# Decode attention over two KV caches: slots of eight heads with 64 KB runs, products in place, one V buffer

## The chip, the cores and the metric

The kernel runs on one core of one Trainium2 chip. The metric is the device time of one execution in microseconds (us); lower is better. The kernel before takes 2577.59 us (median of 3 runs, 2576.91 to 2578.84).

## The reference

Two independent attention blocks, A and B, of the same shapes; their outputs stand side by side. All data are bf16. There is one query token per batch, so each byte of K and V is used once.

```python
B, Sq, D = 8, 1, 1024
H, Sk, Dh = 32, 4096, 128
q = (x @ wq).reshape(B, Sq, H, Dh).transpose(0, 2, 1, 3)
scores = einsum("bhqd,bhkd->bhqk", q, k_cache) * Dh ** -0.5
p = softmax(scores, axis=-1)
o = einsum("bhqk,bhkd->bhqd", p, v_cache)
y = o.transpose(0, 2, 1, 3).reshape(B, Sq, H * Dh) @ wo      # for A and for B
```

K and V of both blocks are 4 x 268 MB, wq and wo 4 x 8.4 MB.

## The kernel before

The program is built as lists of operations, one for each engine, in the order in which they are added (`Program`). Each operation names what it reads and writes and which PSUM banks it touches; from that the program works out the semaphore waits. An engine does its list in order. Stretches of the lists that repeat are emitted as loops (`rolled`).

**Slots.** The work is cut into slots. A slot is one batch and HP = 4 heads of one block, so there are NS = 128 of them. A head's 4096 tokens are spread over SEG = 32 partitions, T = 128 tokens each; four heads fill the 128 partitions. K of a slot is one DMA of 4 MB: 128 rows, each one run of 32 KB (`load_k`), and V likewise (`load_v`). There are two K buffers and two V buffers. All these DMAs are issued by SP, in the order of the list, each after the readers of its buffer are done.

**Scores.** For each half of a slot's tokens (`ch`, 64 tokens of each partition), DVE multiplies K by the query, which `make_qbc` has spread over the partitions, into `prod` (`multiply`, L348). PE adds 16 groups of 8 columns by matmuls with the identity into the PSUM bank `red` (`add_up`, L358), DVE adds the remaining 8 (`reduce`, L371).

**Softmax.** DVE takes the maximum of each partition, transposes blocks of 32 so that the maximum over a head's 32 partitions can be taken, and scales it (L376 to L381). ACT does four Exp instructions, one for each head on its 32 partitions (L385), which write `prob` and the row sums. `prob` has one column per head and is zero on the other heads' partitions, so that one matmul serves all four heads.

**Output.** `pv` does 32 matmuls, four side by side in column groups of the array, into `oacc` (L416). ACT copies it to `osb` (L405). `gather` adds its strips with the selection matrix `sel` (L438), `rowsum` and `invert` give one over the sum of the exps, and `heads` multiplies the two. After eight slots `permute`, `permuted` and `project` multiply with 512 rows of wo (`load_wo`, 1 MB). The last eight slots are projected at the very end, where V comes in four parts of 1 MB and wo in two.

**Order.** Slot n issues K(n) and V(n-1), multiplies its first half, finishes the second half and the softmax of slot n-1, gathers slot n-2, and does `pv` of slot n-1 last. A slot's chain therefore reaches into the next two slots. At the start the four halves of the two wq are loaded into the V and K buffers.

Of the kernel before, what the change touches and what calls it, by code (L numbers as in the profile page):

```python
# [145 lines left out]
def _build(nc, caches, out):  # L146
# [4 lines left out]
    HP = 4  # L151
# [9 lines left out]
    QT = 4  # L161
    NB = 2
    RS = 4
    assert Sq == 1 and Dh == 128 and Sk == 4096 and D == 1024 and H % HP == 0 and B == 8
    assert RS * H * Dh == T * Dh and R == NB * RS
# [3 lines left out]
    with es:  # L169
# [7 lines left out]

        ident = sb("ident", [128, 128], BF16)
        ones = sb("ones", [128, 128], FP32)
        sel = sb("sel", [128, TB, HP], FP32)  # L180
        xs = sb("xs", [B, NC, D], BF16)
        xT = sb("xT", [128, NC, R, B], BF16)
        qrow = sb("qrow", [128, 2, 512], BF16)
        qT = sb("qT", [128, NC, H * B], BF16)
        qbc = sb("qbc", [128, 2, QT, Dh], BF16)
        kbuf = sb("kbuf", [128, NB, T * Dh], BF16)
        vbuf = sb("vbuf", [128, NB, T * Dh], BF16)
        wob = sb("wob", [128, HP, D], BF16)
        prod = sb("prod", [128, 2, CT * Dh], BF16)
        score = sb("score", [128, 2, T], FP32)  # L190
        prob = sb("prob", [128, 2, T, HP], BF16)
        rmax = sb("rmax", [128, 2], FP32)
        tmax = sb("tmax", [128, 2, SEG], FP32)
        nmax = sb("nmax", [128, 2], FP32)
        bias = sb("bias", [128, 2], FP32)
        rsum = sb("rsum", [128, 2, HP], FP32)
        rl = sb("rl", [128, 2, HP], FP32)
        osb = sb("osb", [128, 2, 512], FP32)
        olate = sb("olate", [128, 2 * Dh], FP32)
        on = sb("on", [128, HP, B], BF16)  # L200
        onp = sb("onp", [128, HP, B], BF16)
        qg = sb("qg", [128, HP, B], BF16)
        pick = sb("pick", [40, 2, B], FP32)
        osum = sb("osum", [40, 512], FP32)
        asb = sb("asb", [40, 512], FP32)
        orow = sb("orow", [40, NC, 512], BF16)

        red = [ps(f"red{i}", [128, 512]) for i in range(2)]
        oacc = [ps(f"oacc{i}", [128, 512]) for i in range(2)]
        acc = ps("acc", [128, 512])  # L210
        accr = ps("accr", [128, 512])
        qps = [oacc[0], oacc[1]]
        bps = ps("bps", [128, 512])
        sps = ps("sps", [128, 512])

# [5 lines left out]
        for c in range(NC):  # L221
            dma("act", xs[:, c, :], caches[c][0].rearrange("b s d -> (b s) d"), [f"xs{c}"], f"x{c}")
# [5 lines left out]
        for j in range(4):  # L228
# [3 lines left out]
        P.add("pool", lambda e: e.memset(pick[:], 0.0), writes=["pick"])  # L232
        P.add("pool", lambda e: e.affine_select(
            out=pick[:], in_=pick[:], compare_op=ALU.not_equal, fill=1.0, base=0,
            pattern=[[-32, 2], [-1, B]], channel_multiplier=1), reads=["pick"], writes=["pick"])
        P.add("dve", lambda e: e.memset(prob[:], 0.0), writes=[f"prob{i}h{h}" for i in range(2) for h in range(HP)])
        P.add("dve", lambda e: e.memset(rsum[:], 0.0), writes=[f"rsum{i}h{h}" for i in range(2) for h in range(HP)])
        P.add("dve", lambda e: e.memset(olate[:], 0.0), writes=["olate"])
        P.add("dve", lambda e: e.memset(ones[:], 1.0), writes=["ones"])
        for i in range(2):  # L240
            P.add("dve", lambda e, i=i: e.memset(oacc[i][:], 0.0), banks=[f"oacc{i}"])
        P.add("dve", lambda e: e.memset(acc[:], 0.0), banks=["acc"])
        P.add("dve", lambda e: e.memset(accr[:], 0.0), banks=["accr"])

        ring = {"k": 0, "v": 0}
        bufs = {"k": kbuf, "v": vbuf}

        def slot(which):
            i = ring[which] % NB
            ring[which] += 1  # L250
            return i

        def load_wq(which, c, s):
            i = slot(which)
            w = bufs[which][:, i, :].rearrange("p (r n) -> p r n", r=RS)
            src = caches[c][3].rearrange("(p r) n -> p r n", r=R)[:, s * RS:(s + 1) * RS, :]
            dma("sp", w, src, [f"{which}{i}"], f"{which}{i}")
            return f"{which}{i}", w

        def make_xT(c):  # L260
            def emit(e):
                last = None
                for r in range(R):
                    last = e.matmul(sps[:, 256 + r * B:256 + (r + 1) * B], xs[:, c, r::R], ident[0:B, 0:B], start=True, stop=True)
                return last
            P.add("pe", emit, reads=[f"xs{c}", "ident"], banks=["sps"])
            P.add("dve", lambda e: e.tensor_copy(xT[:, c].rearrange("p r b -> p (r b)"), sps[:, 256:256 + R * B]),
                  writes=[f"xT{c}"], banks=["sps"])

        def q_part(c, s, name, w):  # L270
            def emit(e):
                last = None
                for r in range(RS):
                    for k in range(8):
                        q = k % 4
                        last = e.matmul(qps[k // 4][32 * q:32 * q + B, :], xT[:, c, s * RS + r, :], w[:, r, k * 512:(k + 1) * 512],  # L276
                                        start=(s == 0 and r == 0), stop=(s == R // RS - 1 and r == RS - 1), tile_position=(0, 32 * q))
                return last
            P.add("pe", emit, reads=[name, f"xT{c}"], banks=["oacc0", "oacc1"])
            if s < R // RS - 1:  # L280
                return
            for k in range(2):
                P.add("dve", lambda e, k=k: e.tensor_copy(qrow[:, k, :], qps[k][:]), writes=[f"qrow{k}"], banks=[f"oacc{k}"])  # L283
# [8 lines left out]
            P.add("pe", turn, reads=["qrow0", "qrow1", "ident"], banks=["bps"])  # L292
            P.add("dve", lambda e: e.tensor_copy(qT[:, c, :], bps[:, 0:H * B]), writes=[f"qT{c}"], banks=["bps"])

        def load_k(n):
            gi, b = divmod(n, B)
            c, g = divmod(gi, NG)
            i = kslot[n] = slot("k")
            src = caches[c][1][b, g * HP:(g + 1) * HP].rearrange("h (p t) d -> (h p) (t d)", t=T)
            dma("sp", kbuf[:, i, :], src, [f"k{i}"], f"k{i}")  # L300

        def load_v(m, parts):
            gi, b = divmod(m, B)
            c, g = divmod(gi, NG)
            i = slot("v")
            src = caches[c][2][b, g * HP:(g + 1) * HP].rearrange("h (p t) d -> (h p) (t d)", t=T)
            w = T * Dh // parts
            names = [f"v{i}"] + [f"vpart{k}" for k in range(1, parts)]
            for k in range(parts):
                dma("sp", vbuf[:, i, k * w:(k + 1) * w], src[:, k * w:(k + 1) * w], [names[k]], names[k])  # L310
            vslot[m] = (i, names)

        def load_wo(gi):
            c, g = divmod(gi, NG)
            src = caches[c][4][g * HP * Dh:(g + 1) * HP * Dh, :]
            if gi < NC * NG - 1:
                dma("sp", wob[:], src.rearrange("(p h) n -> p h n", p=Dh), ["wo"], "wo")
                return
            src = src.rearrange("(h p) n -> p h n", p=Dh)
            for k, name in enumerate(("wo", "wolate")):  # L320
                dma("sp", wob[:, 2 * k:2 * k + 2, :], src[:, 2 * k:2 * k + 2, :], [name], name)

        def pick_q(gi):
            c, g = divmod(gi, NG)
            P.add("pool", lambda e: e.tensor_copy(qg[:].rearrange("p h b -> p (h b)"), qT[:, c, g * HP * B:(g + 1) * HP * B]),
                  reads=[f"qT{c}"], writes=["qg"])

        def make_qbc(n):
            b0 = n % B
            i = (n // QT) % 2  # L330

            def emit(e):
                last = None
                for j in range(QT):
                    for hh in range(HP):
                        last = e.matmul(bps[hh * SEG:(hh + 1) * SEG, j * Dh:(j + 1) * Dh],
                                        qg[:, hh, b0 + j:b0 + j + 1].to_broadcast([128, SEG]), ident[:], start=True, stop=True,
                                        tile_position=(0, hh * SEG))
                return last
            P.add("pe", emit, reads=["qg", "ident"], banks=["bps"])  # L340
            P.add("act", lambda e: e.activation(qbc[:, i].rearrange("p i d -> p (i d)"), bps[:], ACTF.Copy),
                  writes=[f"qbc{i}"], banks=["bps"])

        def multiply(n, ch):
            ki, qi, i = kslot[n], (n // QT) % 2, ch % 2
            pv = prod[:, i, :].rearrange("p (t d) -> p t d", d=Dh)
            kv = kbuf[:, ki, ch * CT * Dh:(ch + 1) * CT * Dh].rearrange("p (t d) -> p t d", d=Dh)
            P.add("dve", lambda e: e.tensor_tensor(  # L348
                pv, kv, qbc[:, qi, n % QT, :].unsqueeze(1).to_broadcast([128, CT, Dh]), ALU.mult),
                reads=[f"k{ki}", f"qbc{qi}"], writes=[f"prod{i}"])  # L350
# [156 lines left out]
        def idle(k):  # L507
            if not k:
                return
# [207 lines left out]
```

## Time and profile before

| | before |
|---|---|
| median of 3 runs | 2577.59 us |
| the profiled execution's own time | 2578.69 us |
| its span | 2576.5 us |
| bytes moved by DMA | 1107.59 MB, mean 430 GB/s |
| share of the span in which the engine is busy | PE 62%, DVE 56%, ACT 15%, POOL 1% |
| multiply (L348), 128 x 8192 elements | 256 times 4420 ns |
| Exp (L385), 32 x 128 elements | 512 times 576 ns |
| mean granted TensorE clock | 0.789 of full speed |

The span is the time from the first to the last instruction of the program in the profile, and the profiled execution's own time lies 2.2 us above it. A row of a group gives the line, the engine, the operation, what is written and read, the shape, and the count; behind the bar stand the busy time in us, the mean duration of one in ns, and the idle time of the engine just before it, with what ended that. In a window's row stand its length, the busy time of PE, PE's weight loads, DVE, ACT and POOL with their counts, the granted clock, the busy share of the DMA engines, and GB/s.

### The profile page before, as it was taken

The numbers are of one execution on the slowest core, as the hardware profiler recorded it, in microseconds if no ns is written. First come the engines' busy times: TensorE is split into PE (matmuls) and PEld (weight loads), VectorE is DVE, ScalarE is ACT, GpSimd is POOL, SyncE is SP. The second block draws the span as 40 slices with busy tenths as digits, with TensorE's granted clock in tenths as the row PEclk, the third lists the DMA queues.
The fourth block names the chain that finished last, engine by engine and source line by source line (L and its number), as shares of the span: only waits on it lengthen the run. The fifth ranks groups of instructions, "written<-read, shape, count | busy, mean of one in ns | idle before, by whom it ended". The sixth has DMA issues, their size and how long they took to land.

```text
span 2576.5 us, 22383 instructions
## 1 busy us (share of the span) xinstructions
PE 1596.0 (62%) x10610; PEld 301.0 (12%) x6770; DVE 1436.4 (56%) x1328; ACT 390.4 (15%) x1187; POOL 22.0 (1%) x44
## 2 busy tenths in 40 slices
PE   3666566656665666666566656665666566666657
PEld 1011111111111111111111111110111101111112
DVE  2655565555555655655565555555655565565555
ACT  0111111111111111111111111111111111111111
POOL 0000000000000000000000000000000000000000
PEclk7787777787787778778778777787878778777788
DMA  9999999999999999999999999999999999999998
GB/s 418 432 431 431 431 432 432 431 431 431 432 430 434 431 431 432 431 431 431 432 432 431 432 431 431 431 431 432 431 431 431 432 431 431 432 431 431 433 432 378
DMA packets 40688, 1107.59 MB, mean 430 GB/s; under 512 B 4528, under 2 KB 4560, under 8 KB 5088
## 3 DMA queue, kind: packets, MB, share of 16 engines
q1 hardware_dynamic: 40624, 1107.34, 100.0%
q8 instruction: 10, 0.16, 0.0%
q10 hardware_dynamic: 48, 0.04, 0.0%
q14 instruction: 6, 0.05, 0.0%
HBM read 1107.33 MB, written 0.03 MB: 430 GB/s over the span
## 4 chain that ended last, share of the span: by engine, by line
DMA 73%; DVE 15%; issue 10%; PE 1%; DVEq 0%; ACT 0%; SPq 0%
DMA kbuf<-in_B_k_cache_dram 36%; DMA kbuf<-in_A_k_cache_dram 35%; DVE prod L348 12%; DVE score L371 2%; DMA kbuf<-in_B_wq_dram 1%; DVE rmax L376 1%; DMA vbuf<-in_B_v_cache_dram 1%; DVE tmax L377 1%; DVE nmax L379 0%; PE red L358 0%; DVE bias L381 0%; PE oacc L276 0%; DVEq L649 0%; ACT prob L385 0%; SPq L219 0%
## 5 line engine op out<-in xcount | busy, mean ns | idle before, releaser
L358 PE MATMUL red<-prod,ident 128*128 128x512 bf16 x4096 | 1195.5, 458 | 943.2 <-DVE prod L348 943.2
L348 DVE TENSOR_TENSOR prod<-kbuf,qbc 128x8192 bf16<-128x8192 bf16 x256 | 1131.6, 4420 | 944.3 <-DMA kbuf<-in_B_k_cache_dram 472.3
L385 ACT ACTIVATE prob<-score,bias 32x128 bf16<-32x128 f32 x512 | 295.1, 576 | 1078.5 <-DVE bias L381 1067.5
L416 PE MATMUL oacc<-vbuf,prob 128*16 128x512 bf16 x4088 | 252.8, 379 | 0.8 <-DMA vbuf<-in_B_v_cache_dram 0.8
L405 ACT ACTIVATE osb<-oacc 128x512 f32<-128x512 f32 x128 | 76.5, 597 | 1049.5 <-PE oacc L416 1049.5
L438 PEld LDWEIGHTS sps<-sel,osb 128*128 128x128 f32 x1024 | 134.3, 191 | 666.7 <-issue 514.8
L371 DVE TENSOR_REDUCE score<-red 128x64 f32<-128x512 f32 x256 | 175.6, 686 | 26.4 <-PE red L358 25.7
L358 PEld LDWEIGHTS red<-prod,ident 128*128 128x128 bf16 x256 | 35.1, 137 | 1008.1 <-DVE prod L348 1008.0
L416 PEld LDWEIGHTS oacc<-vbuf,prob 128*16 128x16 bf16 x4088 | 93.8, 89 | 477.6 <-issue 383.8
L385 ACT ACTIVATION_READ_ACCUMULATOR prob<-score,bias 32x1 f32 x512 | 128.0, 250 | 0.0
L438 PE MATMUL sps<-sel,osb 128*128 128x4 f32 x1024 | 121.9, 242 | 0.1
L392 PE MATMUL sps<-rsum,ones 128*128 128x4 f32 x256 | 47.0, 254 | 1.1 <-ACT prob L385 1.1
L476 DVE COPY asb<-acc 40x512 f32<-40x512 f32 x15 | 10.2, 682 | 61.3 <-PE acc L471 61.3
L447 DVE TENSOR_TENSOR on<-sps,rl 128x4 bf16<-128x4 f32 x128 | 22.1, 173 | 35.0 <-PE sps L392 23.2
L392 PEld LDWEIGHTS sps<-rsum,ones 128*128 128x128 f32 x256 | 38.8, 191 | 8.9 <-ACT prob L385 8.7
L376 DVE TENSOR_REDUCE rmax<-score 128x1 f32<-128x128 f32 x128 | 36.6, 286 | 4.4
L480 POOL TENSOR_TENSOR osum<-asb,osum 40x512 f32<-40x512 f32 x12 | 15.1, 1256 | 1881.0 <-DVE asb L476 1881.0
L377 DVE STREAM_TRANSPOSE tmax<-rmax 128x32 f32<-128x32 f32 x128 | 27.0, 211 | 4.5
L379 DVE TENSOR_REDUCE nmax<-tmax 128x1 f32<-128x32 f32 x128 | 23.9, 187 | 4.4
L283 DVE CAST qrow<-oacc 128x512 bf16<-128x512 f32 x4 | 2.6, 686 | 35.5 <-PE oacc L276 35.5
L397 DVE RECIPROCAL rl<-sps 128x4 f32<-128x4 f32 x128 | 22.2, 173 | 0.0
L381 DVE TENSOR_SCALAR bias<-nmax 128x1 f32<-128x1 f32 x128 | 19.6, 154 | 4.4
(57 smaller groups left out, 128.3 us busy)
## 6 DMA issues: line engine op xcount, KB each, us to landing
kbuf<-in_A_k_cache_dram SPq DMA_DIRECT2D x64, 4096.0 KB, 28.5
vbuf<-in_A_v_cache_dram SPq DMA_DIRECT2D x64, 4096.0 KB, 32.3
kbuf<-in_B_k_cache_dram SPq DMA_DIRECT2D x64, 4096.0 KB, 28.5
vbuf<-in_B_v_cache_dram SPq DMA_DIRECT2D x63, 4096.0 KB, 32.3
vbuf<-in_A_wq_dram SPq DMA_DIRECT2D x2, 4096.0 KB, 16.8
kbuf<-in_B_wq_dram SPq DMA_DIRECT2D x2, 4096.0 KB, 36.9
wob<-in_A_wo_dram SPq DMA_DIRECT2D x8, 1024.0 KB, 30.6
wob<-in_B_wo_dram SPq DMA_DIRECT2D x7, 1024.0 KB, 30.6
```

What stands on the lines that cost most here:

```text
L348: P.add("dve", lambda e: e.tensor_tensor(pv, kv, qbc[:, qi, n % QT, :].unsqueeze(1).to_broadcast([128, CT, Dh]), ALU.mult), reads=[f"k{ki} ...
L358: first = e.matmul(rv, ident[:], pj[:, :, 0, :], start=True, stop=False).ins
L371: P.add("dve", lambda e: e.tensor_reduce(dst, rv, AX.X, ALU.add), writes=[f"score{n % 2}c{ch}"], banks=[f"red{i}"])
L376: P.add("dve", lambda e: e.tensor_reduce(rmax[:, i:i + 1], score[:, i, :], AX.X, ALU.max), reads=sc, writes=[f"rmax{i}"])
L377: P.add("dve", lambda e: e.transpose(tmax[:, i, :], rmax[:, i:i + 1].to_broadcast([128, SEG])), reads=[f"rmax{i}"], writes=[f"tmax{i}"])
L379: P.add("dve", lambda e: e.tensor_reduce(nmax[:, i:i + 1], tmax[:, i, :], AX.X, ALU.max), reads=[f"tmax{i}"], writes=[f"nmax{i}"])
L385: P.add("act", lambda e, pr=pr, hh=hh: e.activation(prob[pr, i, :, hh], score[pr, i, :], ACTF.Exp, bias=bias[pr, i:i + 1], scale=scale, ac ...
L392: P.add("pe", lambda e: e.matmul(sps[:, i * HP:(i + 1) * HP], ones[:], rsum[:, i, :], start=True, stop=True), reads=[f"rsum{i}h{h}" for h ...
L397: P.add("dve", lambda e: e.reciprocal(rl[:, i, :], sps[:, i * HP:(i + 1) * HP]), writes=[f"rl{i}"], banks=["sps"])
L405: P.add("act", lambda e: e.activation(osb[:, i, :], oacc[i][:], ACTF.Copy), writes=[f"osb{i}"], banks=[f"oacc{i}"])
L416: last = e.matmul(to[32 * q:32 * q + tb * HP, 0:tb * Dh], prob[:, i, t:t + tb, :].rearrange("p t h -> p (t h)"), vbuf[:, vi, t * Dh:(t + t ...
L438: last = e.matmul(sps[:, o:o + HP], of, sel[:, t, :], start=(t == 0 and not late), stop=(t == tb - 1 and (late or parts == 1)))
```

## The change

A slot takes eight heads: SEG = 16 partitions and T = 256 tokens for each head, K and V of a slot are 8 MB in rows of 64 KB, and there are 64 slots. A slot has four chunks of 64 tokens per partition. The products are written over K itself, in the K buffer. There is one V buffer, one `prob`, one `score` (which lies in the same memory as `osb`). Each of eight Exp instructions works on all 128 partitions with a bias column of its own, in which `neg` holds -1e30 for the partitions of the other heads. A slot now runs from its first multiply to its softmax, `gather` of the slot before, `rowsum` and `invert` before the next slot starts; `pv` of slot n-1 follows slot n's sums. wo comes in loads of 512 KB for two heads, every second slot, and the last eight heads' wo in four loads at the end. V of the last slot comes in parts of 4, 2, 1 and 1 MB into a K buffer. The loops have a body of two slots. The wq are loaded whole, one into the V buffer, one into the second K buffer.

```diff
-    HP = 4
+    HP = 8
...
+        kbuf = sb("kbuf", [128, 2, T * Dh], BF16)
+        vbuf = sb("vbuf", [128, T * Dh], BF16)
+        wob = sb("wob", [128, 2, D], BF16)
+        prob = sb("prob", [128, T, HP], BF16)
+        osb = sb("osb", [128, TB * Dh], FP32)
...
-        kbuf = sb("kbuf", [128, NB, T * Dh], BF16)
-        vbuf = sb("vbuf", [128, NB, T * Dh], BF16)
-        wob = sb("wob", [128, HP, D], BF16)
-        prod = sb("prod", [128, 2, CT * Dh], BF16)
...
+        score = osb[:, 0:T]
+        wlast = vbuf[:, 0:HP * D].rearrange("p (h n) -> p h n", h=HP)
...
+        def load_k(n):
+            c, g, b = where(n)
+            dma("sp", kbuf[:, n % 2, :], source(c, 1, b, g), [f"k{n % 2}"], f"k{n % 2}")
+
+        def load_v(m):
+            c, g, b = where(m)
+            if m < NS - 1:
+                dma("sp", vbuf[:], source(c, 2, b, g), ["v"], "v")
+                vplace[m] = (vbuf[:], [("v", 0, T)])
+                return
...
+        def load_wo(p):
+            dma("sp", wob[:], wo_rows(p).rearrange("(p j) n -> p j n", j=2), ["wo"], "wo")
...
         def multiply(n, ch):
...
+            kv = chunk(n, ch).rearrange("p (t d) -> p t d", d=Dh)
             P.add("dve", lambda e: e.tensor_tensor(
-                pv, kv, qbc[:, qi, n % QT, :].unsqueeze(1).to_broadcast([128, CT, Dh]), ALU.mult),
-                reads=[f"k{ki}", f"qbc{qi}"], writes=[f"prod{i}"])
+                kv, kv, qbc[:, n % 2, :].unsqueeze(1).to_broadcast([128, CT, Dh]), ALU.mult),
+                reads=[f"k{n % 2}", "qbc"], writes=[f"prod{n % 2}c{ch}"])
...
+        def exps(n):
+            i = n % 2
+            for h in range(HP):
+                P.add("act", lambda e, h=h: e.activation(
+                    prob[:, :, h], score, ACTF.Exp, bias=bias[:, h:h + 1], scale=scale, accum_out=rsum[:, i, h:h + 1]),
+                    reads=scores + ["bias"], writes=[f"prob{h}", f"rsum{i}h{h}"])
...
+        def copy_o(m):
+            P.add("act", lambda e: e.activation(osb[:], oacc[:], ACTF.Copy), writes=scores, banks=["oacc"])
...
+            load_k(n)
+            if p is not None:
+                load_wo(p)
+                pick_heads(p)
+            if m >= 0:
+                load_v(m)
+            if n % 2 == 1 and n + 1 < NS:
+                pick_q(n + 1)
+            multiply(n, 0)
+            add_up(n, 0)
+            multiply(n, 1)
+            if p is not None:
+                permute()
+            reduce(n, 0)
+            if p is not None:
+                permuted()
+            add_up(n, 1)
+            multiply(n, 2)
+            if p is not None:
+                project()
+            reduce(n, 1)
+            add_up(n, 2)
+            multiply(n, 3)
+            reduce(n, 2)
+            if p is not None:
+                projected(p)
+            add_up(n, 3)
+            reduce(n, 3)
+            softmax(n)
+            if m >= 0:
+                pv(m)
+            if n % 2 == 1 and n + 1 < NS:
+                make_qbc(n + 1)
+            if n == NS - 1:
+                load_v(n)
+                load_wo_last()
+                idle(32)
+            exps(n)
+            if m >= 0:
+                copy_o(m)
+                gather(m)
+                heads(m)
+            rowsum(n)
+            invert(n)
```

Here m = n - 1, and p counts the projections of two heads each. `chunk(n, ch)` is the part of K buffer n % 2 that holds chunk ch, and `source` the 128 rows of eight heads in K or V.

## The prediction

> **What bounds the kernel now.** I read the page first, then the windows, then the timelines of one slot. The page:
>
> ```profile
> span 2576.5 us, 22383 instructions
> PE 1596.0 (62%) x10610; PEld 301.0 (12%) x6770; DVE 1436.4 (56%) x1328; ACT 390.4 (15%) x1187; POOL 22.0 (1%) x44
> ...
> DMA packets 40688, 1107.59 MB, mean 430 GB/s; under 512 B 4528, under 2 KB 4560, under 8 KB 5088
> ...
> DMA 73%; DVE 15%; issue 10%; PE 1%; DVEq 0%; ACT 0%; SPq 0%
> ...
> L358 PE MATMUL red<-prod,ident 128*128 128x512 bf16 x4096 | 1195.5, 458 | 943.2 <-DVE prod L348 943.2
> L348 DVE TENSOR_TENSOR prod<-kbuf,qbc 128x8192 bf16<-128x8192 bf16 x256 | 1131.6, 4420 | 944.3 <-DMA kbuf<-in_B_k_cache_dram 472.3
> ```
>
> No engine is over 62% busy, and DVE's first multiply of a slot waits for K (944.3 us in all). The windows of two slots, without and with a load of wo:
>
> ```profile
> 1503.70:1542.55 38.85, 24.65 (x172) 4.86 (x112) 22.88 (x22) 5.83 (x18) 0.76 (x2) 0.82 1.00 432
> 1542.55:1583.88 41.33, 24.09 (x164) 4.58 (x104) 22.09 (x20) 6.31 (x19) 0.00 (x0) 0.79 1.00 431
> ```
>
> The last two numbers of each are the DMA share, 1.00, and 432 and 431 GB/s. So the time is bytes over rate, and three things alone can move it: what a DMA costs besides its bytes, stretches in which the queue is empty, and the two ends. The timeline of a slot gives the durations of the sum:
>
> ```profile
> 1523.27 4.42 DVE L348 TENSOR_TENSOR prod<-kbuf,qbc 128x8192 bf16<-128x8192 bf16 x1 [3.28 <-DMA kbuf<-in_B_k_cache_dram]
> 1527.61 0.68 DVE L371 TENSOR_REDUCE score<-red 128x64 f32<-128x512 f32 x1
> 1527.75 5.66 PE L358 MATMUL red<-prod,ident 128*128 128x512 bf16 x16 [6.76 <-DVE prod L348]
> ...
> 1534.28 3.61 PE L358 MATMUL red<-prod,ident 128*128 128x512 bf16 x16
> ...
> 1537.83 1.90 PE L416 MATMUL oacc<-vbuf,prob 128*16 128x512 bf16 x32
> 1539.78 0.60 ACT L405 ACTIVATE osb<-oacc 128x512 f32<-128x512 f32 x1 [8.08 <-PE oacc L416]
> 1539.82 0.33 SPq L219 DMA_DIRECT2D vbuf<-in_B_v_cache_dram  x1
> ```
>
> The first sum of a slot, after some 7 us of idle PE, takes 5.66 us (four in a row: 5.66, 6.18, 5.02, 6.00; mean 5.7), the next 3.61; V is asked for 0.04 us after its last reader.
>
> **Part one: fewer, larger DMAs (bytes unchanged).** Multiplies of chunk 0 start 19.43 us apart, and 21.91 us apart where a wo load (1 MB) lies between. So a 4 MB load takes 19.43 / 2 = 9.715 us and a 1 MB load 2.48 us: a straight line through both has 2.412 us per MB and (4 x 2.48 - 9.715) / 3 = 0.068 us that does not depend on size. Both loads have the same 128 rows, of 32 KB and 8 KB, so the 0.068 us goes with a DMA or its rows, and a load of 128 rows of 64 KB should pay it once for 8 MB: 19.36 us instead of 19.43. Large loads before: 4 wq, 128 K, 127 + 4 V, 15 + 2 wo = 280. After: 2, 64, 63 + 4, 28 + 4 = 165. 115 x 0.068 = 7.9 us less. Rows of 64 KB are in no row of this trace. Bounds: nothing saved, and even +1 us for the 15 more wo loads, if a row is moved as two; 10.6 us, if each engine's 32 KB and 8 KB packets are read alone (1.217 and 0.313 us: 0.0116 us each besides bytes, 8 of them per load). I take 7.9, which is throughput.
>
> The distance of the rows doubles too, from 32 to 64 KB. The wq loads already have rows 64 KB apart (32 KB of each are taken): in the timeline the first matmuls on them start at 12.92 and 22.64, 9.72 us for 4 MB, so nothing is lost. [...]
>
> **Part two: one chain through a slot.** Before, a slot's second half overlaps the next slot's start. After, multiply(n+1, 0) stands behind invert(n) on DVE, so a slot's chain C must be shorter than its DMA time, 2 x 19.36 + 1.27 / 2 = 39.35 us (a wo load of 0.5 MB every second slot, by the line 0.068 + 0.5 x 2.412 = 1.27 us). From multiply 0 at 0: PE's first sum starts at 4.48 and takes 5.7 -> 10.2. reduce 0 (0.6) -> multiply 2 at 10.9; reduce 1 and multiply 3 at 10.9 + 4.34 + 0.61 = 15.85 (the second sum, 3.61, is done at 13.8); last sum 20.3 to 23.95. pv: 64 matmuls where 32 took 1.90; 3.5 us -> 27.4. The maxima (0.42 + 0.21 + 0.19 + 0.16, with reduce 3: exps ready at 25.8) lie beside it, but exps(n) writes the one prob that pv(n-1) reads, so it waits for 27.4. Eight exps: start to start 0.61 us at 128 elements; ACT's copies of 256 and 512 elements (the groups) take 0.385 and 0.597, 0.83 ns per element, so 0.72 at 256, 5.75 in all -> 33.2. copy_o 0.60 -> 33.8. gather: 0.95 warm, taken up to twice that on a PE idle since 27.4 -> 34.8 to 35.7; heads, rowsum, invert and the start of the next multiply 0.9 -> 35.7 to 36.6. Odd slots add make_qbc before the exps (PE 0.35, ACT 0.4), even ones permuted on DVE (0.2): C is 36 to 37.4. It hides under 39.35 with 2 to 3 us over. In place multiplication is in no row; the nearest is the same shape into prod, 4.42 us, from below no reason for less, above it each 0.1 us is 0.4 us of C; I take 4.42. PE's permute and project and DVE's projected (0.45) lie in the 1.5 us holes before the sums and before reduce 3. Queues: load_wo stands on SP between load_k and load_v and waits for project of two slots before; POOL's copies have a slot of slack. Loop ends (DVE 0.35 us from the last instruction to the next) come every two slots instead of eight, inside the margin.
>
> **Part three: one V buffer.** load_v(n) now waits for pv(n-1), and load_k(n+2) is queued behind it on SP. In the steady state that is 27.4 us after K(n) landed, and V(n-1) and K(n+1) keep the queue full until 38.7: 11 us of cover. Once it fails. Loads without a wait: wq, wq, K(0), K(1), V(0), then K(2) (its buffer is free at 85). The first 4 MB land at 12.92, so the queue starts at 12.92 - 9.72 = 3.2, and they land at 22.6, 41.9, 61.2, 80.6, 99.9 and 119.3. Slot 0 starts at 61.2 and lasts 32.2 (no pv to wait for, no gather); slot 1 starts at 93.4 and pv(0) ends at 120.8. Only then is V(1) issued; the first issue of the program took 3.2 - 0.74 = 2.46 us to flow, so the queue is dry from 119.3 to 123.3: +4.1 us (3.2 to 5 with the first sums at 5.0 to 6.2; 2 if the restart is faster than the start). One slot later V(2) is issued at about 158, K(3) lasts until 162: full again, and the slots gain on K by 2 to 3 us each. The Trainium skill (Trainium Kernel Development and Optimization, Best Practices) asks for double buffers to overlap DMA and compute; by it each slot would lose what slot 1 loses, which is the first rival below, and the 11 us speak against it.
>
> **Part four: the end.** Before, the last wo half (issued 2554.74, in the queue behind the last V) lands near 2571.9 and the span ends 4.6 us later: gather, heads, project in four groups, cast, store. After, the last V parts land 5.2 us before the last of four wlast loads (0.5 MB, 1.3 us each), so gather and heads (2.5 us before) are done; left are 8 matmuls 0.7, the DVE sum 0.45, one more DMA issue 0.35, store 2.0: 3.6 us. -1.0 (0 to -1.5; +1 if PE has gone slow).
>
> **Sum.** 2576.5 - 7.9 + 4.1 - 1.0 = 2571.7 us of span. The profiled execution took 2578.69, 2.2 more than its span, and the median is 1.1 below it: 2572.8, 0.19% less. About 0.2%, 5.2 us, is what a measurement of this kernel tells from no change, so the forecast lies on that edge; its own range is 2568 to 2577.
>
> **Rivals.** One, slower: C exceeds 39.2 us (from slot 1 at 93.4 to K(63) at about 2522: 62 slots). Then DVE never catches up, V and K are issued late every slot, and each us costs 62: at C = 40 2572.8 + 0.8 x 62 = 2622. For it: the chain now crosses four engines in series, with PE slow twice in it. Against: it needs 2 us that no row shows; 0.5 us more per multiply in place would do it. 10%. Two: the 0.068 us goes with 32 KB rows, because 64 KB is moved as two: no saving, 1 us for wo, the gap stays: 2577.6 + 1 + 4.1 - 1 = 2581.7. 10%. Three: the saving is 10.6 by packets, or the gap is 1 to 2 (fast restart, first sums at 5.0): 2567 to 2570. 20%. Four: rows 64 KB apart with 64 KB runs slow the reads; 1% would be 127 x 0.19 = 25 us, 2597. The wq row speaks against. 5%.
>
> **How the numbers follow.** The forecast has 55%: half of it beyond 0.2%, half within, a trace slower. Rival three is nearly all faster, two mostly within, one and four slower. Faster 0.27 + 0.19 = 0.46; same 0.27 + 0.01 + 0.08 = 0.36; slower 0.18. The range goes from 2566 (rival three) to 2583 (rival two and the forecast's bad end); rival one and four and a few per cent below are left out.
>
> **What would show it.** Right: starts of chunk 0's multiply 38.7 and 40.0 us apart, each after 2 to 3 us of idle DVE that K's DMA ends; a dry queue near 119 to 123 us and nowhere else; 4.42 us per multiply; the last landing 3.6 us before the end. Wrong: 38.85 between multiplies (no saving), DVE waiting for PE or ACT rather than K at the slot's start (rival one), a gap that returns each slot, or packets of 32 KB.

## The result and the profile after

The kernel after takes 2692.68 us (median of 6 runs, 2691.60 to 2693.91) where before takes 2577.47: 1.0447 times as long, 95% interval 1.0433 to 1.0460. It is slower by 115 us; the forecast was 2572.8. The page of after, the lines that answer to those shown of before:

```profile
span 2690.5 us, 19432 instructions
PE 1493.6 (56%) x9521; PEld 294.5 (11%) x5681; DVE 1381.2 (51%) x965; ACT 647.6 (24%) x1122; POOL 48.5 (2%) x165
...
DMA packets 24445, 1107.54 MB, mean 412 GB/s; under 512 B 2720, under 2 KB 2784, under 8 KB 7408
...
PE 38%; DVE 31%; ACT 22%; issue 7%; DMA 2%; another core or an unknown queue 0%; DVEq 0%; SPq 0%; ACTq 0%
...
L350 DVE TENSOR_TENSOR kbuf<-kbuf,qbc 128x8192 bf16<-128x8192 bf16 x256 | 1124.8, 4414 | 17.0 <-DMA kbuf<-in_A_k_cache_dram 11.3
L388 ACT ACTIVATE prob<-osb,bias 128x256 bf16<-128x256 f32 x512 | 598.5, 1582 | 1034.5 <-PE oacc L411 979.8
...
L388 ACT ACTIVATION_READ_ACCUMULATOR prob<-osb,bias 128x1 f32 x512 | 252.6, 493 | 0.0
```

The chain that ended last was 73% DMA; now DMA has 2% of it, and PE, DVE and ACT share it. DVE's multiply, which waited 944 us for K, waits 17 us in all, 11 of them for the first K: from slot 1 on K is always there first. ACT went from 390 to 648 us of work, and an Exp with its sum from 576 + 250 ns to 1582 + 493 ns (the two overlap). The timeline of one slot, from the end of pv to the next slot's multiplies:

```profile
1560.36 1.43 ACT L388 ACTIVATE prob<-osb,bias 128x256 bf16<-128x256 f32 x1 [30.62 <-PE oacc L411]
1560.40 0.33 SPq L225 DMA_DIRECT2D vbuf<-in_B_v_cache_dram  x1
...
1561.32 1.60 ACT L388 ACTIVATE prob<-osb,bias 128x256 bf16<-128x256 f32 x1
...
1562.45 1.60 ACT L388 ACTIVATE prob<-osb,bias 128x256 bf16<-128x256 f32 x1
...
1569.76 0.60 ACT L427 ACTIVATE osb<-oacc 128x512 f32<-128x512 f32 x1
1570.41 1.78 PEld L437 LDWEIGHTS sps<-sel,osb 128*128 128x128 f32 x8 [10.59 <-ACT osb L427]
1570.41 1.88 PE L437 MATMUL sps<-sel,osb 128*128 128x8 f32 x8 [10.10 <-ACT osb L427]
...
1573.54 8.76 DVE L350 TENSOR_TENSOR kbuf<-kbuf,qbc 128x8192 bf16<-128x8192 bf16 x2 [0.16 <-issue]
```

Exp starts every 1.13 us; eight of them and the copy end 10 us after pv, PE stands idle for all of it, and the next multiply follows 3.2 us later without waiting for K. This slot began at 1532.68: it took 40.86 us. The starts of all slots from slot 1 on are 40.96 us apart in the mean, against 39.35 us of DMA time. V is asked for at 1560.40, and the K load ahead of it, the last in the queue, lands at 1560.52. V lands 21.92 us behind that K, where 8 MB take 19.35 in a full queue, so the queue stands still for some 2.5 us. In the other slots a load of wo still lies behind K, and 0.8 us are lost; the mean is 1.7 us in a slot. Two slots in windows (length; busy time and instructions of PE, PEld, DVE, ACT and POOL; granted clock, DMA share and GB/s):

```profile
1478.00:1519.20 41.20, 22.98 (x147) 4.32 (x80) 21.36 (x14) 9.96 (x17) 0.53 (x2) 0.79 0.96 411
1519.20:1560.30 41.10, 23.41 (x156) 4.60 (x92) 21.66 (x16) 10.22 (x18) 1.05 (x3) 0.79 0.98 417
```

This is the first rival: the slot's chain has become the bound. The experiments ask whether the chain is the cause, or the one V buffer; why the Exp is so long; and whether the rest of the prediction stands when the chain is short.

### The profile page after: what moved, and what is told of

Its sections match the earlier page's. It is cut to its first block, busy times and chain, and to the rows that moved or that the text cites. A ratio compares the mean times of both kernels' runs of the same rounds, so it can differ in the third digit from the quotient of the medians.

```text
span 2690.5 us, 19432 instructions
## 1 busy us (share of the span) xinstructions
PE 1493.6 (56%) x9521; PEld 294.5 (11%) x5681; DVE 1381.2 (51%) x965; ACT 647.6 (24%) x1122; POOL 48.5 (2%) x165
## 4 chain that ended last, share of the span: by engine, by line
PE 38%; DVE 31%; ACT 22%; issue 7%; DMA 2%; another core or an unknown queue 0%; DVEq 0%; SPq 0%; ACTq 0%
DVE kbuf L350 28%; PE red L360 23%; ACT prob L388 21%; PE oacc L411 9%; PE sps L437 4%; DVE osb L372 2%; DMA kbuf<-in_B_wq_dram 2%; PE sps L394 1%; ACT osb L427 1%; DVE on L450 0%; PE bps L338 0%; DVE onp L469 0%; DVE rl L400 0%; PE oacc L269 0%
## 5 line engine op out<-in xcount | busy, mean ns | idle before, releaser
L360 PE MATMUL red<-kbuf,ident 128*128 128x512 bf16 x4096 | 1064.9, 421 | 492.2 <-DVE kbuf L350 492.2
L350 DVE TENSOR_TENSOR kbuf<-kbuf,qbc 128x8192 bf16<-128x8192 bf16 x256 | 1124.8, 4414 | 17.0 <-DMA kbuf<-in_A_k_cache_dram 11.3
L388 ACT ACTIVATE prob<-osb,bias 128x256 bf16<-128x256 f32 x512 | 598.5, 1582 | 1034.5 <-PE oacc L411 979.8
L437 PE MATMUL sps<-sel,osb 128*128 128x8 f32 x512 | 118.4, 360 | 637.1 <-ACT osb L427 637.0
L372 DVE TENSOR_REDUCE osb<-red 128x64 f32<-128x512 f32 x256 | 175.7, 686 | 294.1 <-PE red L360 294.1
L388 ACT ACTIVATION_READ_ACCUMULATOR prob<-osb,bias 128x1 f32 x512 | 252.6, 493 | 0.0
L411 PE MATMUL oacc<-vbuf,prob 128*32 128x512 bf16 x4032 | 229.1, 380 | 0.0
L411 PEld LDWEIGHTS oacc<-vbuf,prob 128*32 128x32 bf16 x4032 | 101.5, 97 | 314.7 <-issue 218.2
L394 PE MATMUL sps<-rsum,ones 128*128 128x8 f32 x128 | 37.9, 370 | 27.6 <-DVE on L450 16.3
L427 ACT ACTIVATE osb<-oacc 128x512 f32<-128x512 f32 x64 | 38.2, 597 | 8.9 <-PE oacc L411 6.7
```

What stands on the lines that cost most here:

```text
L350: P.add("dve", lambda e: e.tensor_tensor(kv, kv, qbc[:, n % 2, :].unsqueeze(1).to_broadcast([128, CT, Dh]), ALU.mult), reads=[f"k{n % 2}", ...
L360: first = e.matmul(rv, ident[:], pj[:, :, 0, :], start=True, stop=False).ins
L372: P.add("dve", lambda e: e.tensor_reduce(score[:, ch * CT:(ch + 1) * CT], rv, AX.X, ALU.add), writes=[f"score{ch}"], banks=[f"red{i}"])
L388: P.add("act", lambda e, h=h: e.activation(prob[:, :, h], score, ACTF.Exp, bias=bias[:, h:h + 1], scale=scale, accum_out=rsum[:, i, h:h + 1]),
L394: P.add("pe", lambda e: e.matmul(sps[:, i * HP:(i + 1) * HP], ones[:].to_broadcast([128, 128]), rsum[:, i, :], start=True, stop=True), rea ...
L411: last = e.matmul(to[32 * q:32 * q + tb * HP, 0:tb * Dh], prob[:, t:t + tb, :].rearrange("p t h -> p (t h)"), buf[:, t * Dh:(t + tb) * Dh] ...
```

## The experiments

**1. Half of the Exp left out.** Four heads of each slot are not computed; their part of `prob` is set to zero once, at the start.

```diff
-            for h in range(HP):
+            for h in range(HP // 2):
                 P.add("act", lambda e, h=h: e.activation(
```

> After with four of the eight Exp of each slot left out (their heads' columns stay zero, so those heads are not computed). Theory chain: the slot's chain of 40.96 us is the bound because it is longer than the 39.35 us that its DMAs take; four Exp less make it 36.4, DVE waits for K again, and the time falls to 2568 to 2582. Rival buffer: the single V buffer empties the DMA queue in every slot whatever the chain's length; the time stays above 2640.

Measured: 2571.95 us, 0.9976 of before (0.9966 to 0.9986). DVE's multiply waits for K again, 191 us in all, and slots start 38.7 and 39.97 us apart:

```profile
DVE kbuf L352 <- DMA kbuf<-in_B_k_cache_dram: 98.2, 32, 4.7
...
DVE kbuf L352 <- DMA kbuf<-in_A_k_cache_dram: 92.7, 28, 10.3
```

So the chain is the cause, and one V buffer is enough once the chain is short.

**2. The chain cut elsewhere, every Exp as slow as in after.**

```diff
             multiply(n, 0)
-            add_up(n, 0)
             multiply(n, 1)
+            if m >= 1:
+                heads(m - 1)
+            if m >= 0:
+                invert(m)
+            add_up(n, 0)
...
                 gather(m)
-                heads(m)
             rowsum(n)
-            invert(n)
```

> After with heads(n-1) and invert(n) moved on DVE behind the first two multiplies of slot n+1, nothing else changed. Theory chain: the multiplies then run while ACT does the Exp, the chain between two slots falls from 40.96 to some 36 to 37 us with every Exp as slow as now, the slots wait for K and the time is 2569 to 2582. Rival buffer: V is asked for at the same point of the chain, the queue still runs dry in every slot, and at best the 4.5 us of the multiply come off for the first slots: above 2640.

Measured: 2573.90 us, 0.9985 of before (0.9976 to 0.9995), with the Exp unchanged at 1582 ns. So it is not the Exp as such but its place in a serial slot: DVE now multiplies while ACT works, and K's loads end its waits.

```profile
DVE kbuf L350 <- DMA kbuf<-in_B_k_cache_dram: 432.4, 32, 14.8
...
DVE kbuf L350 <- DMA kbuf<-in_A_k_cache_dram: 393.6, 30, 14.9
```

These waits are 826 us, where after had 11. Two single instructions of DVE, `heads` and `invert`, moved behind two others are worth 119 us.

**3. What the Exp's time is made of.** Three kernels that do nothing but Exp on ACT, each form twelve times in a row.

> Measures Exp on ACT by itself; no attention is computed, the output is zeros. Twelve Exp in a row for each of fourteen forms, which differ in partitions, elements, distance of the written elements, sum over the elements, and the bias. Start to start, before had 0.61 us (32 x 128, written 8 B apart) and after has 1.13 us (128 x 256, written 16 B apart). Theory distance: the cost grows with the distance of the bf16 results, so 128 x 256 takes 0.65 to 0.80 us with the results side by side, about 0.9 at 8 B and 1.13 at 16 B, whatever the partitions. Theory partitions: 32 x 256 takes about 0.7 and 128 x 256 about 1.13 at every distance. Theory length: 256 elements take 1.0 or more at every distance and every number of partitions. Theory bias: 1.13 only with the bias of -1e30.

The groups of that kernel (name, partitions x elements; mean ns of one behind the busy time): pa and pb have results 8 B apart at 128 elements, pc and pd 8 B at 256, pl, pe and pf 16 B at 256, pf with the bias of -1e30, pg side by side, pn in runs of four.

```profile
L186 ACT ACTIVATE pf<-score,bias 128x256 bf16<-128x256 f32 x12 | 17.3, 1440 | 0.4
L186 ACT ACTIVATE pl<-score,bias 32x256 bf16<-32x256 f32 x12 | 17.2, 1437 | 0.4
L186 ACT ACTIVATE pe<-score,bias 128x256 bf16<-128x256 f32 x12 | 17.1, 1424 | 0.4
...
L186 ACT ACTIVATE pd<-score,bias 128x256 bf16<-128x256 f32 x12 | 10.3, 860 | 0.4
L186 ACT ACTIVATE pc<-score,bias 32x256 bf16<-32x256 f32 x12 | 10.3, 859 | 0.4
...
L186 ACT ACTIVATE pa<-score,bias 32x128 bf16<-32x128 f32 x12 | 6.9, 576 | 0.4
L186 ACT ACTIVATE pb<-score,bias 128x128 bf16<-128x128 f32 x12 | 6.9, 575 | 0.4
...
L186 ACT ACTIVATE pg<-score,bias 128x256 bf16<-128x256 f32 x12 | 6.3, 523 | 0.4
L186 ACT ACTIVATE pn<-score,bias 128x256 bf16<-128x256 f32 x12 | 6.1, 506 | 0.4
```

Partitions change nothing (pa, pb; pc, pd; pl, pe), nor does the bias (pe, pf). The length explains little: side by side, 256 elements take 523. The distance of the results explains it: start to start 0.63 us at 2 B, 0.90 at 8 B, 1.46 at 16 B, where 1.13 was expected (more on this below). The change had doubled both the heads, and with them the distance from 8 to 16 B, and the elements.

> Exp on ACT by itself again; no attention is computed, the output is zeros. 128 x 256 with bf16 results 3, 4, 6, 8 and 16 elements apart, 64 and 512 elements at 8 apart, and float32 results 1, 4 and 8 elements apart. Theory bytes spanned: the pitch follows the distance in bytes beyond 4, about 0.9 us at 8 B, 1.18 at 12, 1.46 at 16, 2.6 at 32, and float32 at 4 elements apart (16 B) costs as much as bf16 at 16 B. Rival single writes: every distance from 8 B on costs the same per element, and only the number of results counts.

Measured, start to start at 256 elements: 0.66 us at 4 B (from the kernel above), 0.76 at 6, 0.90 at 8, 1.18 at 12, 1.47 at 16, but 1.42 at 32 B; at 16 B 0.63 for 64 elements and 2.61 for 512; float32 results 0.63 side by side, 0.78 at 16 B, 0.79 at 32 B. The lines of bf16 at 16 B (pd) and 32 B (pe) and of float32 at 16 B (qb):

```profile
L184 ACT ACTIVATE pd<-score,bias 128x256 bf16<-128x256 f32 x12 | 17.2, 1430 | 0.4
L184 ACT ACTIVATE pe<-score,bias 128x256 bf16<-128x256 f32 x12 | 16.5, 1378 | 0.4
...
L189 ACT ACTIVATE qb<-score,bias 128x256 f32<-128x256 f32 x12 | 8.9, 741 | 0.4
```

Both expectations missed: the cost grows only to 16 B, and float32 hardly shows it. From 6 B on, the bf16 values lie within 0.05 us of 0.34 + 0.0044 for each line that the results touch, a line being a stretch of 16 B in SBUF (256 lines: 1.47; 192: 1.18; 128: 0.90; 512: 2.59). That is a fit, no mechanism: float32 at 16 B touches 256 lines too and takes 0.78.

The Trainium skill (SBUF — State Buffer, Door 1: The DMA port swizzle) says that SBUF works in lines of 16 bytes and each access that crosses to a new line pays a penalty; the growth up to 16 B and the halt there agree. It calls a distance of 8 bf16 or 4 fp32 free: here 8 bf16 cost 2.3 times the time of results side by side, 4 fp32 1.2 times.

> Exp on ACT by itself a third time; no attention is computed, the output is zeros. 128 x 256 with bf16 results 16 B apart, into three tiles at different places, from two sources, with the bias and sum columns changing from one Exp to the next as in the kernel. In the kernel after, such an Exp took 1.13 us, alone 1.46. Theory place: the pitch depends on where the tile or the source lies, and some pairs show 1.13. Theory columns: all six groups show 1.13, because bias and sum change. Theory surroundings: all six show 1.46, and what makes it shorter in the kernel lies outside the Exp itself.

All six groups gave 1.13 us, so neither place nor source matters:

```profile
4.89 1.60 ACT L178 ACTIVATE one<-sa,b 128x256 bf16<-128x256 f32 x1
...
6.03 1.60 ACT L178 ACTIVATE one<-sa,b 128x256 bf16<-128x256 f32 x1
```

In the two kernels before this one each Exp waited for the end of the one before it, since both wrote the same column of sums by the program's names; here the columns change, as in after. So the 1.46 contains 0.33 us of that wait. That it is the wait and not the bias, the first of these kernels shows where one form follows another. There the column of sums changes, no wait stands between, and the bias column stays; yet the next Exp starts 0.67 us after the last one at 8 B instead of 0.90:

```profile
26.16 0.86 ACT L186 ACTIVATE pc<-score,bias 32x256 bf16<-32x256 f32 x1
...
26.83 0.84 ACT L186 ACTIVATE pd<-score,bias 128x256 bf16<-128x256 f32 x1
```

At 2 B it is 0.51 and at 16 B 0.96 at such a place, so the order of the forms is not affected.

**4. The Exp made short by where it writes.** The same work, but `prob` lies in blocks of four tokens. In a block each of the eight heads has its four results side by side, so an Exp writes runs of 8 B and touches a 16 B line once for four results (the last part of V goes through the same four-token matmuls as the rest):

```diff
-        prob = sb("prob", [128, T, HP], BF16)
+        prob = sb("prob", [128, T // TB, HP, TB], BF16)
...
-                pattern=[[-HP, TB], [-1, HP]], channel_multiplier=1), reads=["sel"], writes=["sel"])
+                pattern=[[-1, TB], [-TB, HP]], channel_multiplier=1), reads=["sel"], writes=["sel"])
...
-                    prob[:, :, h], score, ACTF.Exp, bias=bias[:, h:h + 1], scale=scale, accum_out=rsum[:, i, h:h + 1]),
+                    prob[:, :, h, :], score.rearrange("p (a t) -> p a t", t=TB), ACTF.Exp, bias=bias[:, h:h + 1], scale=scale, accum_out=rsum[:, i, h:h + 1]),
```

> After with prob laid out in blocks of four tokens, so that an Exp writes runs of four results (8 B) 64 B apart instead of single results 16 B apart; the selection matrix follows, and the last part of V goes through four-token matmuls. Theory distance by single writes: an Exp falls to 0.75 to 0.9 us, the chain to 37.5 to 39.1, and the time to 2570 to 2590. Theory distance by bytes spanned, and the theories of partitions, length and bias: the Exp stays at 1.1 us and the time at 2685 to 2697.

Measured: 2571.47 us, 0.9974 of before (0.9963 to 0.9985). The Exp fell below what either theory said, to 495 ns, 0.49 us from start to start:

```profile
L388 ACT ACTIVATE prob<-osb,bias 128x256 bf16<-128x256 f32 x512 | 252.1, 495 | 1124.1 <-PE oacc L411 1069.5 <-DVE bias L381 54.6
```

and the timeline of DVE shows the slots waiting for K at 39.98 and 38.71 us, as the prediction has them:

```profile
1300.61 8.76 DVE L350 TENSOR_TENSOR kbuf<-kbuf,qbc 128x8192 bf16<-128x8192 bf16 x2 [3.62 <-DMA kbuf<-in_B_k_cache_dram]
1340.59 8.76 DVE L350 TENSOR_TENSOR kbuf<-kbuf,qbc 128x8192 bf16<-128x8192 bf16 x2 [4.17 <-DMA kbuf<-in_B_k_cache_dram]
1379.30 8.76 DVE L350 TENSOR_TENSOR kbuf<-kbuf,qbc 128x8192 bf16<-128x8192 bf16 x2 [3.71 <-DMA kbuf<-in_B_k_cache_dram]
```

**5. What larger loads are worth, taken by itself.** Version 4, each load of 8 MB split:

```diff
+        def two(dst, src, name):
+            for x, at in (("a", 0), ("b", HALF)):
+                dma("sp", dst[:, at:at + HALF], src[:, at:at + HALF], [name + x], name + x)
...
-            dma("sp", kbuf[:, n % 2, :], source(c, 1, b, g), [f"k{n % 2}"], f"k{n % 2}")
+            two(kbuf[:, n % 2, :], source(c, 1, b, g), f"k{n % 2}")
```

> The version with blocked prob (2571.47 us), with each of its 129 loads of 8 MB issued as two loads of 4 MB with rows of 32 KB, nothing else changed. Theory fixed cost: a load pays 0.068 us whatever its size, so 129 more loads cost 129 x 0.068 = 8.8 us: 2580, with 38.85 us between slots without wo instead of 38.70. Rival: the row length does nothing and the gain lies at the ends: 2571 to 2573, 38.70.

Measured: 2581.56 us, 1.0017 of before (1.0008 to 1.0026), so 10.1 us above version 4. Slots without wo are 38.86 us apart in the mean instead of 38.71:

```profile
1346.21 8.76 DVE L356 TENSOR_TENSOR kbuf<-kbuf,qbc 128x8192 bf16<-128x8192 bf16 x2 [4.48 <-DMA kbuf<-in_B_k_cache_dram]
...
1385.09 8.76 DVE L356 TENSOR_TENSOR kbuf<-kbuf,qbc 128x8192 bf16<-128x8192 bf16 x2 [2.42 <-DMA kbuf<-in_B_k_cache_dram]
```

With two further loads in a slot that is 0.075 us for each, and 129 x 0.075 = 9.7. The rival falls. Whether the cost sits in the load or in its rows (128 of 32 KB for each) is not parted by this.

**6. The dry queue at the start.** Version 4, and pv(0) pulled ahead in slot 1, so that V(1) is asked for earlier:

```diff
             reduce(n, 1)
+            if n == 1:
+                pv(0)
             add_up(n, 2)
...
-            if m >= 0:
+            if m >= 1:
                 pv(m)
```

> The version with blocked prob, with pv(0) on PE after the second sum of slot 1 instead of after its fourth (the loops start two slots later for it). V(1) is then asked for at about 111 us, before K(2) has landed at 120.7. Theory start gap: the DMA queue no longer runs dry there (the load that lands at 144.28 after 23.60 us takes 19.35) and 3 to 4.3 us come off: 2567 to 2568.5. Rival: the gap only moves to V(2), and the time stays at 2571 to 2572.

Measured: 2568.48 us, 0.9966 of before (0.9952 to 0.9979). The windows from 100 to 125 us, first of version 4, then of this one: the DMA share goes from 0.82 to 0.97.

```profile
100.00:125.00 25.00, 18.22 (x127) 2.01 (x69) 14.65 (x11) 3.77 (x16) 0.00 (x0) 0.96 0.82 343
```

```profile
100.00:125.00 25.00, 18.51 (x131) 3.05 (x74) 14.28 (x11) 5.02 (x18) 0.00 (x0) 0.91 0.97 417
```

V(1) landed 4.25 us late in version 4 (23.60 us behind the load ahead of it, where 19.35 are usual). Of these, 3.0 came off the time. K(2) and V(2) still land 0.5 and 0.7 us late. V(2) is asked for 5.2 us before the load ahead of it lands, which is more than the 2.5 to 3.9 us that V took to flow when the queue was dry (after; version 4). So the gap of the rival is not what delays it, and the cause is not shown.

**7. All three together.**

> Blocked prob, early pv(0), and heads and invert of DVE behind the first two multiplies of the next slot, all together. Theory: with the queue full from the first load to the last and the Exp short, 2567 to 2568.5; the deferral adds nothing once the slot waits for K, except that slot 2 asks for V(2) a few us earlier. Rival: as the early version or worse, because rowsum and the first sums of the next slot now share PE.

Measured: 2568.56 us, 0.9965 of before (0.9952 to 0.9979): the same as version 6. From slot 2 on its slots start 38.7 us apart with no gap, so the 0.7 us of V(2) are gone. They are lost again at the end, where the first of the last four wo loads takes 2.15 us instead of the 1.46 of version 6; why is not shown. Both beat before by 0.34%, and the change as it was made by 4.6%.

## Why the prediction was wrong

The step that failed is one line of part two, "Eight exps: start to start 0.61 us at 128 elements; ACT's copies of 256 and 512 elements [...], so 0.72 at 256". Measured 1.13, and 8 x 0.41 = 3.3 us. With the price per element of a copy that writes side by side, the Exp's row was stretched to twice the elements, though its own results lie apart and the change moves them further apart. The step also named no upper bound, as the steps on the loads, the multiply and gather did. Twice the time of the Exp's own row is 1.22 us; with it C becomes 40 to 41.4, above the 39.35 that the DMAs give, and rival one could not have been left at a tenth. The rest of C held, slot for slot: second multiply pair at 11.0 (10.9 said), last sum done at 24.1 (23.95), pv at 27.6 (27.4); gather took 1.88, the slow end of what was given. In the slot shown above, 9.40 us pass from the first Exp to the copy, where 5.75 were said: that is 3.65 of the 4.3 us between 36.6 and 40.9, and the rest are small parts.

The mechanism of the first rival was right and so was its price. 62 slots at 40.96 instead of 39.17 us (from 93.4 to 2522) are 111 us. Slot 1 began 5.2 us later (98.6 for 93.4): slot 0, with the same eight Exp, took 35.85 us instead of 32.2, and K(0) landed at 62.7 instead of 61.2. The prediction had spaced the first loads evenly, though the timeline of before shows 11.4 us, not 9.7, between the second and the third part of the wq (22.64 and 34.02). The end took 2.5 us longer. Together that is the 118.8 us between the span said and the span measured. What was misjudged is the rival's chance: "it needs 2 us that no row shows" was held against it, but no row showed an Exp of that form either, so the rows could not speak against it.

The other terms held where the chain is short. The 0.068 us per load: 0.075 in experiment 5, K and V landing 19.35 us apart (19.36 said). Rows of 64 KB cost nothing beyond that and are moved whole: packets fell from 40688 to 24445. The in place multiply takes 4414 ns (4420). The start gap: 4.25 us in version 4 (4.1 said). The end: 3.4 us behind the last landing in experiment 1 (3.6). With the Exp short (experiments 1 and 4), 2571.5 to 2572.0 us were measured for the forecast of 2572.8.

## What to carry to other kernels

When a change takes the overlap out of the compute and counts on a queue of loads as the only bound, add up the whole serial chain of a slot and hold it against the time of its loads. Here the loads gave 39.35 us, and a margin of 2 to 3 us hung on eight instructions. A duration may only be carried to another size from a row with the same access pattern, and if the pattern changes too, the term needs an upper bound of its own. Where a chain is too long, look first for a short instruction that keeps a long one from starting (two on DVE here), and then for where results are written.

## What the runs showed of the hardware that was not expected

An Exp on ACT with bf16 results slows down with the distance of the results: 256 of them take 0.63 us side by side and 1.46 us at 16 B apart (1.13 without a wait between them), and no more at 32 B. Runs of 8 B bring back 0.63. float32 results at 16 B take 0.78. The number of partitions (32 or 128) and the value of the bias did not matter.
